# Attention features, mixture of experts and SoLU on one core: k and q stacks split in pairs of 64 partitions, and the upper part of k's features on another engine

## The chip, the core and the metric

The kernel runs on one core of a Trainium2 chip. The core has five engines with queues of their own: TensorE (PE, matrix multiplications, with weight loads shown as PEld), VectorE (DVE), ScalarE (ACT), GpSimd (POOL) and SyncE (SP, which here issues all transfers). The metric is device time in microseconds (us) of one execution; lower is better.

## What is computed

Three layers follow one another: random-feature attention over 4 batches of 8 heads, 576 positions and 64 dimensions with 128 features; a mixture of 8 experts in which each token takes one expert; and a SoLU layer with a layer norm.

```python
scale = 1.0 / np.sqrt(np.sqrt(D))
q_s, k_s = (q * scale, k * scale)
def phi(x):
    proj = np.einsum('bhsd,md->bhsm', x, omega)
    h = proj - np.sum(x * x, axis=-1, keepdims=True) / 2.0
    h = h - np.max(h, axis=-1, keepdims=True)
    return np.exp(h) / np.sqrt(m)
q_p, k_p = (phi(q_s), phi(k_s))
kv = np.einsum('bhsm,bhsd->bhmd', k_p, v)
z = np.sum(k_p, axis=2)
num = np.einsum('bhsm,bhmd->bhsd', q_p, kv)
den = np.einsum('bhsm,bhm->bhs', q_p, z)[..., None] + 1e-06
x = (num / den)          # then rows of 512: experts, then SoLU
```

The matrix products run in 16-bit floats, and every factor is split in an upper part (the value rounded to 16 bits) and a lower part (the rest), so that three products give nearly the precision of 32 bits.

## The kernel before, in words

There are three phases. Phase A is the attention, phase B the experts, phase C the SoLU layer. A and B are interleaved by hand: the program is one list of instructions for each engine, in the order in which the code is written (the pool manager orders nothing), and a piece of A is put between the steps of B.

Phase A (`stream_a`) is a list of units. A batch has nine k units (positions in four blocks of 128 and a tail, for two halves of the heads) and nine q units. The text calls one turn of the loop a slot, and it handles several units at once, each at another stage. In slot i, `feat_max` (DVE, tile `nm`) takes the maxima of unit i, `proj` (PE, tile `pj`) makes unit i + 1, `feat_exp` (ACT, tile `feat`, four instructions) makes the features of unit i, and `k_split` divides the features of unit i - 1, when it is a k unit, in `fh` (upper part) and `fl` (lower part); `k_acc` multiplies them with v on PE in slot i + 1. A q unit is transposed on PE instead, split by `q_split`, multiplied in `q_num` and divided in `q_norm`. Between batch 0 and batch 1 lie six slots without units (`GAP`).

`proj` takes its factors from stacks (tile `stk`): 128 partitions, of which 0 to 63 hold the upper and 64 to 127 the lower part of k or q of a pair of heads, in 1152 columns (two heads of 576 positions). One matrix product over the 128 partitions so takes both parts. A stack is made in three steps for batches 1 to 3. `load_pair` (lines 113 to 125) loads the pair from memory twice, once to each half of the partitions. `split_pair` (lines 127 to 139) first casts all of it to 16 bits on ACT (line 138), and then POOL subtracts, on the lower half alone, the cast from the loaded value (line 139, which stands at line 62 in the profile, in the helper `sub`). Batch 0 has its data in another layout and does not come to these lines. There are eight stacks a batch, four of k and four of q, so 24 in all. A table in `stream_a` (lines 387 to 397) says in which slot a stack is split: q of a batch in its slots 1, 3, 5, 7, k of the next batch in slots 11, 13, 15, 17 (six or seven more in batch 0). The load of the pair after next is put two slots behind each.

Phase B (`phase_b`) is a pass over one expert a batch: 16 passes of twelve products (lines 659 to 661) and eight of 24 (lines 676 to 678). ACT and DVE take their results out (`hh`, `hl`, lines 635 and 636; `yT`). Its weights come in 64 chunks (tile `wraw`, three buffers), each split by ACT (`wh`, line 546) and DVE (`wl`, line 547).

SP issues in program order. An instruction of SP that waits holds back all that stand behind it.

Of the kernel before, what the change touches and what calls it, by code (L numbers as in the profile page):

```python
# [8 lines left out]
F32 = mybir.dt.float32  # L9
F32R = mybir.dt.float32r  # L10
F16 = mybir.dt.float16
# [49 lines left out]
def sub(eng, out, a, b):  # L61
    eng.tensor_tensor(out=out, in0=a, in1=b, op=ALU.subtract)  # L62
# [3 lines left out]
def attn_moe_solu(ctx: ExitStack, tc, qk0, qT, kT, v, omT, w_gate, w1, w2, w_in, w_out, g_ln, out):  # L66
# [46 lines left out]
    def load_pair(b, which, pr):  # L113
        if b >= B:
            return
        if b == 0:
            n, cs = "qk".index(which), slice(512 * pr, min(512 * pr + 512, 4 * S))
            raws[b, which, pr] = raw0[n][:, cs]
            sp.dma_start(raws[b, which, pr], qk0[n, :, cs])
            return  # L120
        src = (qT if which == "q" else kT)[b - 1]
        r = ap_.tile([128, 2 * S], F32, name="raw", tag="raw", bufs=2)
        sp.dma_start(r[0:64], src[:, pr, :])
        sp.dma_start(r[64:128], src[:, pr, :])
        raws[b, which, pr] = r

    def split_pair(b, which, pr, fast=False):
        if b >= B:
            return
        dst = stacks[b, which, pr] = ap_.tile([128, 2 * S], F16, name="stk", tag="stk", bufs=8)  # L130
        r = raws.pop((b, which, pr))
        eng = dve if fast else pool
        if b == 0:
            n = r.shape[1]
            act.copy(dst[:, 0:n], r)
            sub(eng, dst[:, S:S + n], r, dst[:, 0:n])
        else:
            act.copy(dst, r)  # L138
            sub(eng, dst[64:128], r[64:128], dst[64:128])

    vraws = {}

# [76 lines left out]
    kvs = {}  # L219
    kvacc = {}  # L220

    def k_split(f):
        h, l = split_feat(f)
        dve.tensor_scalar(h, f, PSC, None, op0=ALU.mult)
        yield h, l
        dve.scalar_tensor_tensor(l, f, PSC, h, op0=ALU.mult, op1=ALU.subtract)  # L226

# [145 lines left out]
    def stream_a():  # L373
# [8 lines left out]
        def at(i, fn):  # L382
            later.setdefault(i, []).append(fn)

        for b in range(B):
            o = U * b + (GAP if b else 0)
            g = 0 if b else GAP
            stream = [(b, "q", i) for i in range(4)] + [(b + 1, "k", i) for i in range(4)]
            stream += [(b + 1, "q", i) for i in range(2)]
            for i in range(8):  # L390
                w = 2 * i + 1 if i < 4 else 2 * i + 3 + g + (b == 0 and i == 4)
                if b == 0 and i < 4:
                    continue
                if stream[i][0] < B:
                    at(o + w, lambda x=stream[i]: split_pair(*x))
                if (b or i >= 4) and stream[i + 2][0] < B:
                    at(o + w + 2, lambda x=stream[i + 2]: load_pair(*x))
            if b == 0:
                for i in range(5):
                    at(QS[i], lambda i=i: split_pair(0, "q", i))  # L400
                at(o + 7 + g, lambda x=stream: (load_pair(*x[4]), load_pair(*x[5])))
            if b + 1 < B:
                for i in range(5):
                    at(o + g + (7, 7, 7, 14, 15)[i], lambda b=b, i=i: load_v(b + 1, i))
                    at(o + g + (11 + (b == 0), 12, 13, 15, 16)[i], lambda b=b, i=i: split_v(b + 1, i))
                    at(o + g + (12 + (b == 0), 13, 14, 16, 17)[i], lambda b=b, i=i: split_v_lo(b + 1, i))
# [27 lines left out]
        while i < n or later or xq or xps or hls or routes:  # L434
# [55 lines left out]
            if i < n and units[i]:  # L490
                feats[i] = feat_exp(pj, nm)
            if unit(i - 1, "k"):
                ks = k_split(feats.pop(i - 1))
                hls[i - 1] = next(ks)
            if new_num:
                b, _, t, half = un
# [686 lines left out]
```

## Time and profile before

| | us |
|---|---|
| median of 3 runs | 569.41 (568.27 to 570.55) |
| the profiled execution | 571.53 |
| its span, first to last instruction | 569.6 |
| PE busy | 507.8 (89%) |
| DVE busy | 454.0 (80%) |
| ACT busy | 336.5 (59%) |
| POOL busy | 121.6 (21%) |
| chain that ended last | PE 45%, DVE 28%, ACT 13%, issue 7%, DMA 4% |

The span has two parts. Up to about 350 us the phases A and B run interleaved, and no engine is busy all the time; from 360 us on, PE is busy nearly without a break with phases B and C. Busy times are read stage by stage, since a share over the whole span mixes the two. A wait is put down to the work that came last before it, and the busy time of an instruction also has in it what held it up while it ran.

### The profile page before, as it was taken

Reading aid. Unit: us, or ns where it says so; the run is one execution under the profiler, and the core shown is the slowest. Engines: PE = TensorE matmul, PEld = TensorE weight load, DVE = VectorE, ACT = ScalarE, POOL = GpSimd, SP = SyncE. Lnnn points to the kernel's source line nnn. Section 1 sums busy time; section 2 is a strip of 40 time slices with the busy share of each in tenths; the row PEclk is TensorE's granted clock in tenths of the full one; section 3 lists DMA queues with packets and bytes.
Section 4 is the critical chain, followed back from the end, with each engine's and each line's share of the span. In section 5 each row is a group of like instructions: output and inputs, shape, how many; then the busy total and the mean of one; then the engine's idle time right before and its main releaser. Section 6 shows DMA issues by size and latency. Waiting matters only on the chain.

```text
span 569.6 us, 11746 instructions
## 1 busy us (share of the span) xinstructions
PE 507.8 (89%) x4440; PEld 344.5 (60%) x4440; DVE 454.0 (80%) x929; ACT 336.5 (59%) x742; POOL 121.6 (21%) x110
## 2 busy tenths in 40 slices
PE   6878677988868998979989978999999999999995
PEld 3656566767757887858867756664444444444443
DVE  6978999889987989786886787777779988878670
ACT  6668656788557885657565456434375646645520
POOL 4221333133330232310011233211112121211100
PEclk9999899999979999989998999999999999999998
DMA  7505744747554454611455545506678887676541
GB/s 255 149 18 175 221 99 102 197 100 201 149 151 117 112 163 124 181 57 57 143 158 174 165 130 184 166 2 145 182 164 229 177 229 164 161 211 150 148 111 43
DMA packets 72462, 83.48 MB, mean 147 GB/s; under 512 B 42192, under 2 KB 42832, under 8 KB 72400
## 3 DMA queue, kind: packets, MB, share of 16 engines
q1 hardware_dynamic: 72400, 82.68, 53.2%
q8 instruction: 36, 0.59, 0.5%
q14 instruction: 26, 0.21, 0.1%
HBM read 63.79 MB, written 9.44 MB: 129 GB/s over the span
## 4 chain that ended last, share of the span: by engine, by line
PE 45%; DVE 28%; ACT 13%; issue 7%; DMA 4%; SPq 1%; POOL 1%; ACTq 0%; DVEq 0%; POOLq 0%
DVE wl L547 5%; PE h L732 5%; PE o L799 5%; PE o L801 5%; PE o L800 5%; PE h L730 5%; PE h L731 5%; ACT feat L211 4%; DVE nm L205 3%; PE g L677 3%; PE g L676 3%; PE g L678 3%; DVE fl L226 2%; ACT wh L546 2%; ACT stk L138 2%
## 5 line engine op out<-in xcount | busy, mean ns | idle before, releaser
L211 ACT ACTIVATE feat<-pj,nm 128x128 f32<-128x128 f32 x288 | 82.8, 378 | 43.5 <-DVE nm L205 39.9
L62 POOL TENSOR_TENSOR stk<-raw,stk 64x1152 f16<-64x1152 f32 (+2 forms) x33 | 68.4, 2073 | 177.6 <-ACT stk L138 141.5
L659 PE MATMUL g<-xh,wh 128*128 128x288 f16 (+2 forms) x224 | 65.2, 291 | 15.0 <-DVE hl L636 13.9
L676 PE MATMUL g<-hh,wh 128*128 128x288 f16 (+2 forms) x256 | 73.4, 287 | 1.1 <-DVE hl L636 0.9
L677 PE MATMUL g<-hl,wh 128*128 128x288 f16 (+2 forms) x256 | 73.5, 287 | 0.4 <-DVE hl L636 0.4
L678 PE MATMUL g<-hh,wl 128*128 128x288 f16 (+2 forms) x256 | 73.5, 287 | 0.0
L547 DVE SCALAR_TENSOR_TENSOR wl<-wraw,wh 128x512 f16<-128x512 f32 x56 | 58.3, 1040 | 16.6 <-ACT wh L546 14.0
L661 PE MATMUL g<-xh,wl 128*128 128x288 f16 (+2 forms) x224 | 65.3, 292 | 0.0
L660 PE MATMUL g<-xl,wh 128*128 128x288 f16 (+2 forms) x224 | 65.3, 292 | 0.0
L799 PE MATMUL o<-woh,lh 128*128 128x512 f16 (+1 forms) x152 | 55.9, 368 | 0.3 <-ACT ob L802 0.3
L801 PE MATMUL o<-woh,ll 128*128 128x512 f16 (+1 forms) x152 | 55.9, 368 | 0.0
L800 PE MATMUL o<-wol,lh 128*128 128x512 f16 (+1 forms) x152 | 55.9, 368 | 0.0
L205 DVE TENSOR_REDUCE nm<-pj 128x4 f32<-128x512 f32 x72 | 49.0, 681 | 0.9 <-PE pj L191 0.8
L636 DVE SCALAR_TENSOR_TENSOR hl<-g,hh 128x288 f16<-128x288 f32 (+2 forms) x64 | 28.9, 452 | 19.1 <-ACT hh L635 18.7
L732 PE MATMUL h<-wih,yl 128*128 128x512 f16 x112 | 42.5, 379 | 0.9 <-POOL yl L62 0.9
L730 PE MATMUL h<-wih,yh 128*128 128x512 f16 x112 | 42.5, 379 | 0.0
L731 PE MATMUL h<-wil,yh 128*128 128x512 f16 x112 | 42.4, 379 | 0.0
L756 POOL TENSOR_TENSOR rs<-sc,neghalf 128x1 f32<-128x1 f32 x18 | 10.3, 573 | 148.1 <-DVE sc L754 148.1
L546 ACT ACTIVATE wh<-wraw 128x512 f16<-128x512 f32 x56 | 36.1, 644 | 4.2 <-PE g L677 4.2
L635 ACT ACTIVATE hh<-g 128x288 f16<-128x288 f32 (+2 forms) x64 | 26.7, 425 | 19.5 <-PE g L661 19.5
L827 ACT ACTIVATE wck<-wck 128x2048 f32<-128x2048 f32 x16 | 30.5, 1904 | 12.6 <-DMA wck<-in_w_dram 12.6
L660 PEld LDWEIGHTS <-wh 128*128 128x128 f16 x224 | 22.2, 99 | 22.9 <-issue 17.5
(181 smaller groups left out, 1251.8 us busy)
## 6 DMA issues: line engine op xcount, KB each, us to landing
wck<-in_w_dram SPq DMA_DIRECT2D x16, 1024.0 KB, 6.0
wraw<-in_w_dram SPq DMA_DIRECT2D x56, 256.0 KB, 2.8
raw<-in_kT_dram SPq DMA_DIRECT2D x24, 288.0 KB, 4.7
raw<-in_qT_dram SPq DMA_DIRECT2D x24, 288.0 KB, 4.6
out_dram<-ob SPq DMA_DIRECT2D x17, 256.0 KB, 2.2
vraw<-in_v_dram SPq DMA_DIRECT2D x16, 256.0 KB, 4.8
xd<-x SPq DMA_DIRECT2D x16, 256.0 KB, 4.6
craw<-in_w_in_dram SPq DMA_DIRECT2D x8, 512.0 KB, 4.0
```

Of the source, the lines that this page charges most:

```text
L211: act.activation(f[:, i, :], ps[:, i, :], AF.Exp, bias=nm[:, i:i + 1])
L547: dve.scalar_tensor_tensor(l, r, BS, h, op0=ALU.mult, op1=ALU.subtract)
L660: pe.matmul(ps, wh[:, c, :], xl[:, c, cs], start=False, stop=False)
L676: pe.matmul(ps, wh[:, k % 4, :], hh[:, k, cs], start=(k == 0), stop=False)
L677: pe.matmul(ps, wh[:, k % 4, :], hl[:, k, cs], start=False, stop=False)
L678: pe.matmul(ps, wl[:, k % 4, :], hh[:, k, cs], start=False, stop=(k == 7))
L730: pe.matmul(ps[:, n, :], h[:, c, :], cw["wih"][:, c, cs], start=(c == 0), stop=False)
L731: pe.matmul(ps[:, n, :], h[:, c, :], cw["wil"][:, c, cs], start=False, stop=False)
L732: pe.matmul(ps[:, n, :], l[:, c, :], cw["wih"][:, c, cs], start=False, stop=(c == 3))
L799: pe.matmul(ps, h[:, k, :], cw["woh"][:, k, cs], start=(k == 0), stop=False)
L800: pe.matmul(ps, h[:, k, :], cw["wol"][:, k, cs], start=False, stop=False)
L801: pe.matmul(ps, l[:, k, :], cw["woh"][:, k, cs], start=False, stop=(k == 7))
```

## The change

Four things change, all of them for batches 1 to 3 alone.

The load: the pair comes once, the first head to partitions 0 to 63, the second to 64 to 127, in 576 columns. There are three buffers of half the size in place of two.

The split: ACT casts 128 x 576 to the first half of a new tile `hlp`, and DVE (no longer POOL) subtracts 128 x 576 into its second half. Four transfers from SBUF to SBUF then put the stack together: for each of the two heads its upper part to partitions 0 to 63, and its lower part to 64 to 127.

The order: the cast stands one slot earlier than the split did, and the subtraction with its four transfers one slot behind the cast. The loads are one slot earlier too.

The features: `fh` of a k unit is made by ACT where DVE made it.

```diff
-        r = ap_.tile([128, 2 * S], F32, name="raw", tag="raw", bufs=2)
-        sp.dma_start(r[0:64], src[:, pr, :])
-        sp.dma_start(r[64:128], src[:, pr, :])
+        r = ap_.tile([128, S], F32, name="raw", tag="raw", bufs=3)
+        sp.dma_start(r[0:64], src[:, pr, 0:S])
+        sp.dma_start(r[64:128], src[:, pr, S:2 * S])
...
-        else:
-            act.copy(dst, r)
-            sub(eng, dst[64:128], r[64:128], dst[64:128])
+            return None
+        hl = ap_.tile([128, 2, S], F16, name="hlp", tag="hlp", bufs=3)
+        act.copy(hl[:, 0], r)
+
+        def rest():
+
+            sub(dve, hl[:, 1], r, hl[:, 0])
+            for o in range(2):
+                for n in range(2):
+                    sp.dma_start(dst[64 * n:64 * n + 64, S * o:S * o + S], hl[64 * o:64 * o + 64, n])
+        return rest
...
-    def k_split(f):
+    def k_split(f, b):
         h, l = split_feat(f)
-        dve.tensor_scalar(h, f, PSC, None, op0=ALU.mult)
+        if b:
+            act.activation(h, f, AF.Copy, scale=PSC)
+        else:
+            dve.tensor_scalar(h, f, PSC, None, op0=ALU.mult)
...
-                w = 2 * i + 1 if i < 4 else 2 * i + 3 + g + (b == 0 and i == 4)
+                w = 2 * i if i < 4 else 2 * i + 2 + g + (b == 0 and i == 4)
...
-                    at(o + w, lambda x=stream[i]: split_pair(*x))
+                    at(o + w, lambda x=stream[i], w=o + w: at(w + 1, split_pair(*x)))
```

Two k slots of batch 1 on DVE, before (`hl`, `wl` and `kvl` are lower parts of phase B's results, of weights and of the sums over k):

```order
L205 TENSOR_REDUCE nm<-pj 128x4
L636 SCALAR_TENSOR_TENSOR hl<-g_1516,hh 128x320
L547 SCALAR_TENSOR_TENSOR wl<-wraw,wh 128x512
L224 TENSOR_SCALAR fh<-feat 128x512
L226 SCALAR_TENSOR_TENSOR fl<-feat,fh 128x512
L250 SCALAR_TENSOR_TENSOR kvl<-kv,kvh 128x260
L205 TENSOR_REDUCE nm<-pj 128x4
L636 SCALAR_TENSOR_TENSOR hl<-g_1572,hh 128x320
L547 SCALAR_TENSOR_TENSOR wl<-wraw,wh 128x512
L224 TENSOR_SCALAR fh<-feat 128x512
L226 SCALAR_TENSOR_TENSOR fl<-feat,fh 128x512
```

The same two slots on DVE after (lines of the new file; the functions further down stand eight to eleven lines lower):

```order
L213 TENSOR_REDUCE nm<-pj 128x4
L647 SCALAR_TENSOR_TENSOR hl<-g_1552,hh 128x320
L558 SCALAR_TENSOR_TENSOR wl<-wraw,wh 128x512
L237 SCALAR_TENSOR_TENSOR fl<-feat,fh 128x512
L261 SCALAR_TENSOR_TENSOR kvl<-kv,kvh 128x260
L213 TENSOR_REDUCE nm<-pj 128x4
L647 SCALAR_TENSOR_TENSOR hl<-g_1607,hh 128x320
L558 SCALAR_TENSOR_TENSOR wl<-wraw,wh 128x512
L62 TENSOR_TENSOR hlp<-raw,hlp 128x576
L237 SCALAR_TENSOR_TENSOR fl<-feat,fh 128x512
```

`fh` is gone from each slot, and the subtraction of a pair stands ahead of `fl` in every second one.

ACT in the same place, before:

```order
L635 ACTIVATE hh<-g_1572 128x320
L546 ACTIVATE wh<-wraw 128x512
L211 ACTIVATE feat<-pj,nm 128x128 x4
L138 CAST stk<-raw 128x1152
L635 ACTIVATE hh<-g_1629 128x320
L546 ACTIVATE wh<-wraw 128x512
L211 ACTIVATE feat<-pj,nm 128x128 x4
```

And after:

```order
L646 ACTIVATE hh<-g_1552 128x320
L557 ACTIVATE wh<-wraw 128x512
L219 ACTIVATE feat<-pj,nm 128x128 x4
L233 ACTIVATE fh<-feat 128x512
L139 CAST hlp<-raw 128x576
L260 ACTIVATE kvh<-kv 128x260
L646 ACTIVATE hh<-g_1607 128x320
L557 ACTIVATE wh<-wraw 128x512
L219 ACTIVATE feat<-pj,nm 128x128 x4
L233 ACTIVATE fh<-feat 128x512
```

`fh` of the unit before stands behind the four `feat` of each slot, and the cast is half as wide.

SP in the first half of batch 1's k slots, before:

```order
L529 DMA wraw<-in_w_dram 128x512
L123 DMA raw<-in_qT_dram 64x1152
L124 DMA raw<-in_qT_dram 64x1152
L123 DMA raw<-in_qT_dram 64x1152
L124 DMA raw<-in_qT_dram 64x1152
L123 DMA raw<-in_qT_dram 64x1152
L124 DMA raw<-in_qT_dram 64x1152
L529 ISA
L529 DMA wraw<-in_w_dram 128x512
```

And after, from the same weight load on:

```order
L540 DMA wraw<-in_w_dram 128x512
L123 DMA raw<-in_qT_dram 64x576
L124 DMA raw<-in_qT_dram 64x576
L146 DMA stk<-hlp 64x576 x4
L123 DMA raw<-in_qT_dram 64x576
L124 DMA raw<-in_qT_dram 64x576
L146 DMA stk<-hlp 64x576 x4
L123 DMA raw<-in_qT_dram 64x576
L124 DMA raw<-in_qT_dram 64x576
L146 DMA stk<-hlp 64x576 x4
L540 ISA
L540 DMA wraw<-in_w_dram 128x512
```

Each stack adds four transfers to SP's queue, of which the first waits for the subtraction. The order on PE does not change, and POOL's list only loses the 24 subtractions.

## Rows read from the trace of the kernel before

**Rows 1.** The page: span, busy times, granted clock in 40 slices.

```profile
span 569.6 us, 11746 instructions
PE 507.8 (89%) x4440; PEld 344.5 (60%) x4440; DVE 454.0 (80%) x929; ACT 336.5 (59%) x742; POOL 121.6 (21%) x110
...
PEclk9999899999979999989998999999999999999998
```

**Rows 2.** Busy time by stage: length, PE, PEld, DVE, ACT, POOL, PEclk, DMA share, GB/s.

```profile
48.30:77.60 29.30, 20.39 (x242) 16.82 (x242) 25.70 (x62) 18.72 (x37) 9.83 (x4) 0.94 0.75 211
77.60:106.00 28.40, 23.30 (x284) 18.31 (x283) 26.70 (x51) 19.77 (x56) 9.49 (x4) 1.00 0.44 112
106.00:136.30 30.30, 25.89 (x324) 22.00 (x325) 25.47 (x56) 24.98 (x65) 7.57 (x4) 1.00 0.65 179
136.30:172.10 35.80, 27.29 (x367) 22.68 (x365) 33.01 (x70) 21.82 (x59) 12.07 (x5) 0.90 0.53 146
172.10:212.00 39.90, 38.34 (x442) 32.73 (x442) 33.59 (x81) 30.91 (x81) 7.67 (x4) 1.00 0.47 127
212.00:251.30 39.30, 33.92 (x444) 28.63 (x443) 33.64 (x77) 24.94 (x66) 11.66 (x5) 1.00 0.46 129
```

**Rows 3.** Single lines on DVE: duration in ns, shortest, median, longest.

```profile
L547 DVE SCALAR_TENSOR_TENSOR wl<-wraw,wh x56: 669/692/2443, 75.5 to 366.7; 128x512 f16<-128x512 f32 x56
...
L224 DVE TENSOR_SCALAR fh<-feat x36: 396/417/1949, 9.2 to 253.3; 128x512 f16<-128x512 f32 x36
...
L205 DVE TENSOR_REDUCE nm<-pj x72: 658/682/694, 7.0 to 285.2; 128x4 f32<-128x512 f32 x72
```

**Rows 4.** Timelines of POOL and of DVE at 102 us: start, duration.

```profile
101.99 2.38 POOL L62 TENSOR_TENSOR stk<-raw,stk 64x1152 f16<-64x1152 f32 x1 [4.97 <-ACT stk L138]
...
102.80 2.11 DVE L547 SCALAR_TENSOR_TENSOR wl<-wraw,wh 128x512 f16<-128x512 f32 x1
```

**Rows 5.** Groups on DVE in the k slots of batch 1, 2, 3 (two rows each).

```profile
L224 DVE TENSOR_SCALAR fh<-feat 128x512 f16<-128x512 f32 x8 | 6.3, 785 | 0.0
L547 DVE SCALAR_TENSOR_TENSOR wl<-wraw,wh 128x512 f16<-128x512 f32 x3 | 4.9, 1633 | 0.1
...
L547 DVE SCALAR_TENSOR_TENSOR wl<-wraw,wh 128x512 f16<-128x512 f32 x5 | 9.8, 1968 | 1.8 <-ACT wh L546 1.7
L224 DVE TENSOR_SCALAR fh<-feat 128x512 f16<-128x512 f32 x8 | 4.8, 602 | 0.1
...
L547 DVE SCALAR_TENSOR_TENSOR wl<-wraw,wh 128x512 f16<-128x512 f32 x8 | 8.6, 1074 | 2.9 <-ACT wh L546 2.8
L226 DVE SCALAR_TENSOR_TENSOR fl<-feat,fh 128x512 f16<-128x512 f32 x8 | 7.1, 893 | 0.4
```

**Rows 6.** Groups of the whole span by shape: busy us, mean ns, idle before.

```profile
L62 POOL TENSOR_TENSOR stk<-raw,stk 64x1152 f16<-64x1152 f32 x24 | 58.3, 2429 | 148.4 <-ACT stk L138 141.5 <-PE pj L200 6.9
L546 ACT ACTIVATE wh<-wraw 128x512 f16<-128x512 f32 x56 | 36.1, 644 | 4.2 <-PE g L677 4.2
L138 ACT CAST stk<-raw 128x1152 f16<-128x1152 f32 x24 | 28.1, 1170 | 0.0
L62 DVE TENSOR_TENSOR tl<-e,th 128x1024 f16<-128x1024 f32 x16 | 19.6, 1225 | 7.0 <-ACT th L782 7.0
```

**Rows 7.** Timelines of DVE and of ACT in one k slot of batch 1.

```profile
98.95 0.68 DVE L205 TENSOR_REDUCE nm<-pj 128x4 f32<-128x512 f32 x1
...
99.73 1.14 ACT L211 ACTIVATE feat<-pj,nm 128x128 f32<-128x128 f32 x4 [2.14 <-DVE nm L205]
```

**Rows 8.** Transfers (KB, median us to landing), SP's issue, and PE's first use.

```profile
raw<-in_qT_dram SPq DMA_DIRECT2D x24, 288.0 KB, 4.6
vraw<-in_v_dram SPq DMA_DIRECT2D x8, 128.0 KB, 4.2
...
102.76 0.60 SPq L124 DMA_DIRECT2D raw<-in_kT_dram  x1
...
104.42 0.23 PE L199 MATMUL pj<-ws,stk 128*128 128x128 f16 x1
```

More of the change, by code (lines that the diff above doesn't have):

```diff
@@ L492, in stream_a @@
             if unit(i - 1, "k"):
-                ks = k_split(feats.pop(i - 1))
+                ks = k_split(feats.pop(i - 1), units[i - 1][0])
                 hls[i - 1] = next(ks)
```

## The prediction

> **What bounds the kernel now.** I read the page first, then busy time by stage, cut where the maxima `nm` of a unit start: the gap (48.3 to 77.6 us), then k and q slots of batches 1, 2 and 3 in turn. The change acts only there; behind it PE runs phases B and C, which the change leaves alone, so a gain made in these stages moves all the rest by as much [rows 1, 2]. In the gap and in the k slots of batches 1 and 2 DVE is busy for 25.7 of 29.3, 26.7 of 28.4 and 33.0 of 35.8 us, with PE at 20.4, 23.3 and 27.3: DVE sets the pace. In the q slots of batch 2 PE is busy for 38.3 of 39.9 us: there nothing that DVE saves comes out. The k slots of batch 3 lie between (PE 33.9 and DVE 33.6 of 39.3), and the q slots of batch 1 load ACT and DVE alike (25.0 and 25.5 of 30.3) [rows 2].
>
> But DVE is not working in all of this busy time. Three lines show it [rows 3]. `wl` takes 692 ns at the median and up to 2443; `fh` takes 417 and up to 1949; `nm`, which reads its values from PE's accumulators and not from SBUF, never takes over 694. The timelines say what holds the long ones: POOL's subtraction for a stack runs from 101.99 to 104.37 us, and the `wl` that starts at 102.80 ends with it, after 2.11 us [rows 4]. So an instruction of DVE that takes two inputs, or one at the fast rate, from SBUF stands still until POOL is done. ACT's cast releases POOL just when ACT turns to the next `wh`, so that `wl` falls in POOL's 2.4 us again and again.
>
> **What goes.** POOL's 24 subtractions of 2.43 us [rows 6], and with them DVE's standstill. By stage, against the medians of rows 3: k slots of batch 1, 8 x (785 - 417) + 3 x (1633 - 692) = 5.8 us; of batch 2, 5 x (1968 - 692) + 8 x (602 - 417) = 7.9; of batch 3, 8 x (1074 - 692) + 8 x (893 - 692) = 4.7 [rows 3, 5]. The gap has four of the 24 too [rows 2]; by batch 1's price they cost 0 to 5.8. The q slots have few hits. DVE also loses 27 `fh` of 417 ns, 11.3 us, nine in each stretch of k slots, and ACT half of each cast: 1170 ns for 1152 columns, about 0.65 for 576, so 12 us over 24 [rows 6].
>
> **What comes, on DVE and ACT.** DVE gets 24 subtractions of 128 x 576. The nearest row is `tl`, the same operation on 1024 columns in 1225 ns; with `wl` at 692 for 512 that is 1.04 ns a column, so 0.76 us each, 18 us in all, 3 in every stage of four pairs [rows 3, 6]. Its bounds are 0.69 (the `wl` of 512) and 1.23. ACT gets 27 `fh`; the nearest row is `wh`, the same shape with a scale, 644 ns, so 17.4 us [rows 6]. Net, DVE has 6.6, 8.7 and 5.5 us less to do in the three stretches of k slots (0.417 x 9 + 5.8, 7.9 or 4.7, less 3), and ACT gets 3.7 more in each (0.644 x 9, less 0.52 x 4).
>
> **The new wait.** `fh` on DVE needed nobody; on ACT it stands behind the four `feat`, and these wait for `nm`. DVE's `fl` now waits for `fh`, and the next `nm` stands behind `fl`. That is one ring for every k slot: `nm` 0.68, hand-over 0.1, `feat` 1.14, `fh` 0.6, `fl` 0.69, in all 3.2 us [rows 3, 5, 7]. While DVE does `fl` and `nm`, ACT has 1.3 us for `hh`, `wh` and the cast; `wh` and the cast take 0.65 each, so when all three come in one slot the ring grows by `hh`, to some 3.6. What now stands between `nm` and `fl` on DVE (`hl`, `wl`, the subtraction) hides under `feat` and `fh`. So no k slot can be shorter than 3.2 us, and this takes back part of what the standstill returns:
> - k slots of batch 1: now 28.4, without standstill 22.6, so the ring sets them. The first of the nine has no k unit before it; eight to nine rings are 25.6 to 28.8, I take 27.4: **-1.0**.
> - of batch 2: now 35.8, without standstill 27.9; nine rings are 28.8, and some slots were over 3.2 anyway: 28.8 to 33, I take 31.5: **-4.3**.
> - of batch 3: now 39.3, without standstill 34.6, and PE alone is busy for 33.9: 34 to 36.5, I take 35.0: **-4.3**.
> - the gap: DVE gets 3 us of subtractions and loses up to 5.8 of standstill; ACT waits for v there too. **-1.5** (-3 to +2).
> - q slots of batch 1: 3 us more on DVE, 2 less on ACT and few hits: **0** (-1 to +2). Of batch 2: PE sets them, DVE has 1.6 us to spare for 3 more: **+0.5** (0 to +2). Of batch 3: no stacks, no change.
>
> **The transfers.** A stack's transit was POOL's 2.4 us. Now DVE's 0.76 is followed by four issues of SP, up to 0.6 each (half-partition transfers in the rows), and by a landing: 4.2 to 4.6 us in the rows of loads from memory [rows 8]; the rows have no transfer inside SBUF, so 2.4 (POOL's own time) to 4.6. From the subtraction's start to the last landing that is 5.6 to 7.8 us. For k stacks and the first three of q there are two slots or more in hand. The fourth stack of q is subtracted in slot 7 and wanted by `proj` in slot 9: two slots of 3.2, 6.4 us, and in batch 1 PE takes its stack at 104.42, 0.05 us behind POOL's end, so without slack already [rows 4, 8]. Price: 0 to 1.4 us a batch, with a busy queue more: **+1.5** (0 to +4). Behind the waiting first transfer on SP stand weight loads. ACT never waited for such a load in 56 times (its idle time before `wh` goes to PE) [rows 6], so SP's extra two microseconds a stack cost nothing while three buffers stand ahead; if that cover were gone, 2 us a stack would come on ACT's path. Transfer load is no matter: the DMA share is 0.44 to 0.75 [rows 2], and the bytes loaded halve while as many are moved inside SBUF.
>
> The Trainium skill speaks against this form. Its page DMA: Bandwidth & Descriptors, section Rules for kernel authors, advises not to cut a transfer in two partition halves, since both use the same 16 engines and serialize; its section Anatomy of one DMA puts a fixed cost of some 2 us on each. By it four would follow one another for about 4 x (2.0 + 0.17) = 8.7 us, an estimate from that page, and the fourth q stack would be some 3 us late in each batch, about 568 in all. Against that, two loads issued 0.6 us apart both land in 4.2 to 4.6 [rows 8], so the fixed part overlaps.
>
> **The sum.** -1.0 - 4.3 - 4.3 - 1.5 + 0.5 + 1.5 = -9.1 us. The profiled execution took 571.53, with a span of 569.6 and so 1.9 outside it; it would become 562.4. It stands 2.1 over the median of the runs shown, 569.41, and by that median the time is **560.3**, say 560.5.
>
> **The rivals.**
> - *The ring doesn't bind, DVE's time comes out whole.* Standstill (18.4 in k slots, 3 in the gap), `fh` (11.3) and casts, less 18 of subtractions: about -18, 551. For it: PE's granted clock averages 0.90 in batch 2's k slots [rows 2], so it stood at the lower level there for a while, and a steadier PE would win that back. Against: the ring follows from the program's order.
> - *Late stacks eat most of it.* Transfers that queue behind loads come 3 us late in each batch at the fourth q stack, or some k stack waits too: +9, 566 to 571. For it: batch 1 has no slack. Against: the q slots of batches 2 and 3 come later.
> - *ACT becomes the bound in k slots: slower.* The place is the 27 k slots. If ACT's `hh`, `wh` and cast do not fit under `fl` and `nm`, and PE's next pass, which waits for `hl`, drifts with them, a slot takes 3.6 plus a wait for PE, about 4.2; 27 x 4.2 = 113 against the 103.5 that these stages take now gives +10, and with gap and lateness 580. It decides from 3.8 us a slot on. For it: ACT would have 25 us of work in 31. Against: ACT's work in a slot, 1.14 + 0.6, `hh` of at most 0.65, and `wh` and the cast in every second slot, is about 3.0.
> - *The standstill doesn't go*, since DVE itself now does the work: no row says that DVE stands for anything but POOL, so I give it no chance of its own.
>
> **How the numbers follow.** The forecast (554 to 566) gets 0.48, whole relief (544 to 554) 0.20, late stacks 0.18, ACT as bound 0.14. About 0.5% is what a measurement of this kernel can tell from no change: under 566.6 is faster, over 572.3 slower. Faster is 0.48 + 0.20 less the slow edge, 0.66; same 0.20; slower 0.14. The range for 8 in 10 leaves out half of whole relief and most of the slow case: 549 to 573. Most of the chance is on one side, so the forecast's own range is the one given with it.
>
> **What would show it.** In the profile after, `wl` and `fh` or `fl` in k slots should have no duration over 0.75 us before phase A ends; DVE's subtraction some 0.76; `fh` on ACT some 0.62, and ACT no longer idle for `nm` but DVE's `fl` idle for `fh`: the ring. The stretches of k slots should take about 27, 31 and 35 us, q slots of batch 2 still about 40. PE waiting for a transfer of `stk` at the tenth or eleventh unit of a batch would show lateness. I am wrong if k slots take over 3.8 us, if PE waits for stacks by over 3 us a batch, or if the subtraction takes over 1.2.

## The result, and the profile after

The changed kernel takes 562.93 us (median of 4 runs, 561.29 to 563.70) against 569.57 before (also 4 runs, 568.27 to 570.55): 0.9874 of the time before, 95% interval 0.9851 to 0.9898, so some 7 us less. The profiled execution took 563.37 us with a span of 561.5.

The page, to be held against [rows 1] (and its line on the transfers: KB, median us to landing):

```profile
span 561.5 us, 11966 instructions
PE 506.7 (90%) x4440; PEld 344.8 (61%) x4440; DVE 432.3 (77%) x926; ACT 339.3 (60%) x769; POOL 63.0 (11%) x86
...
PEclk8998989798999999999999999999999999999999
...
stk<-hlp SPq DMA_DIRECT2D x96, 72.0 KB, 2.3
```

DVE has lost 21.7 us of busy time (454.0 to 432.3) and POOL 58.6; ACT is nearly where it was (336.5 to 339.3), since the 17.5 us of upper parts that it gained are for the most part made up for by the casts, which lost 11.5 (28.1 before [rows 6], 16.6 after). The transfers land 2.3 us after their issue at the median. The groups of DVE and ACT from 0 to 285 us show the parts one by one:

```profile
L237 DVE SCALAR_TENSOR_TENSOR fl<-feat,fh 128x512 f16<-128x512 f32 x36 | 27.3, 758 | 16.3 <-ACT fh L233 15.2
L558 DVE SCALAR_TENSOR_TENSOR wl<-wraw,wh 128x512 f16<-128x512 f32 x37 | 25.6, 691 | 4.1 <-ACT wh L557 2.9 <-DMA stk<-hlp 0.7
L62 DVE TENSOR_TENSOR hlp<-raw,hlp 128x576 f16<-128x576 f32 x24 | 18.0, 750 | 0.2
...
L233 ACT ACTIVATE fh<-feat 128x512 f16<-128x512 f32 x27 | 17.5, 648 | 0.8 <-PE num L286 0.8
L139 ACT CAST hlp<-raw 128x576 f16<-128x576 f32 x24 | 16.6, 690 | 5.0 <-DMA raw<-in_kT_dram 5.0
```

`wl` is back at its own length, 691 ns on average in these stages where it reached 1633 and 1968 in single stretches before [rows 5]; the standstill is gone. In its place `fl` stands idle for 15.2 us until ACT has written `fh`: the ring. The stages, cut where the `nm` of their first unit starts, against [rows 2] (length, PE, PEld, DVE, ACT, POOL, PEclk, DMA share, GB/s):

```profile
48.80:77.20 28.40, 21.10 (x233) 17.17 (x233) 23.48 (x67) 16.61 (x37) 0.00 (x0) 0.88 0.73 220
77.20:104.30 27.10, 23.39 (x283) 18.43 (x281) 20.70 (x46) 22.17 (x64) 0.00 (x0) 1.00 0.52 143
104.30:139.40 35.10, 29.16 (x334) 24.81 (x335) 25.75 (x59) 24.58 (x67) 0.00 (x0) 0.87 0.47 133
139.40:169.70 30.30, 25.52 (x368) 21.83 (x367) 24.89 (x66) 23.09 (x65) 0.00 (x0) 0.98 0.65 184
169.70:210.20 40.50, 38.84 (x444) 32.94 (x444) 34.88 (x83) 30.68 (x83) 0.00 (x0) 1.00 0.45 133
210.20:246.70 36.50, 33.41 (x442) 28.43 (x440) 27.37 (x74) 26.14 (x72) 0.00 (x0) 1.00 0.49 140
```

| stage | before | after | difference | forecast |
|---|---|---|---|---|
| gap | 29.3 | 28.4 | -0.9 | -1.5 |
| k slots, batch 1 | 28.4 | 27.1 | -1.3 | -1.0 |
| q slots, batch 1 | 30.3 | 35.1 | **+4.8** | 0, and a share of the +1.5 for late stacks |
| k slots, batch 2 | 35.8 | 30.3 | -5.5 | -4.3 |
| q slots, batch 2 | 39.9 | 40.5 | +0.6 | +0.5, and a share of the +1.5 |
| k slots, batch 3 | 39.3 | 36.5 | -2.8 | -4.3 |
| all that follows | 318.3 | 314.8 | -3.5 | 0 |

With 0.5 us more ahead of the gap the spans differ by 8.1. One stage went the other way, the q slots of batch 1. Two waits and a lower clock in it are new. SyncE's issues and PE's waits there (start, duration, and in brackets the idle time before):

```profile
100.19 1.38 SPq L157 DMA_DIRECT2D vraw<-in_v_dram  x3
101.68 3.13 SPq L146 DMA_DIRECT2D stk<-hlp  x4
```

```profile
107.21 0.27 PE L207 MATMUL pj<-ws,stk 128*128 128x128 f16 x1 [3.20 <-DMA stk<-hlp]
```

VectorE's subtraction for the fourth q stack ends at 100.5, but SP is issuing three loads of `v`; the four transfers follow from 101.68 on, the last at 104.23, and PE waits 3.20 us for them. From 106.5 on, 0.7 us before that wait ends, the granted clock is at half, which is the level of 1.2 GHz, for 6.8 us, and full again after it (columns as in the stages; the middle row):

```profile
100.00:106.50 6.50, 3.54 (x44) 2.87 (x42) 5.03 (x9) 5.35 (x16) 0.00 (x0) 1.00 0.75 216
106.50:113.30 6.80, 5.87 (x51) 4.93 (x52) 1.38 (x2) 2.28 (x8) 0.00 (x0) 0.50 0.41 125
113.30:120.00 6.70, 6.70 (x73) 5.65 (x72) 5.57 (x12) 6.48 (x19) 0.00 (x0) 1.00 0.29 72
```

The waits of the whole span name SP once more (who waits for whom, us in total, times, longest):

```profile
SPq L146 <- DVE hlp L62: 25.2, 13, 4.5
...
ACT v_h L171 <- DMA vraw<-in_v_dram: 8.6, 5, 2.7
```

SP stands 25.2 us at the transfers until VectorE has subtracted (at the second of each four; the first takes the cast alone), and what is queued behind, the loads of `v` above all, goes out later: ACT waits 8.6 us for `v`. The same waits in the kernel before:

```profile
ACT v_h L163 <- DMA vraw<-in_v_dram: 2.4, 2, 1.3
...
ACT v_h L167 <- DMA vraw<-in_v_dram: 1.6, 1, 1.6
```

### The profile page after: what moved, and what is told of

It is laid out like the page before. It is cut to its first block, busy times and chain, and to the rows that moved or that the text cites. A ratio compares the mean times of both kernels' runs of the same rounds, so it can differ in the third digit from the quotient of the medians.

```text
span 561.5 us, 11966 instructions
## 1 busy us (share of the span) xinstructions
PE 506.7 (90%) x4440; PEld 344.8 (61%) x4440; DVE 432.3 (77%) x926; ACT 339.3 (60%) x769; POOL 63.0 (11%) x86
## 4 chain that ended last, share of the span: by engine, by line
PE 50%; DVE 21%; ACT 11%; DMA 7%; issue 6%; SPq 3%; POOL 1%; ACTq 0%; DVEq 0%; POOLq 0%
PE h L743 5%; PE o L810 5%; PE o L812 5%; PE o L811 5%; PE h L741 5%; PE h L742 5%; ACT feat L219 4%; DVE nm L213 4%; PE g L687 3%; PE g L688 3%; PE g L689 3%; PE g L670 2%; PE g L672 2%; PE g L671 2%; DMA vraw<-in_v_dram 2%
## 5 line engine op out<-in xcount | busy, mean ns | idle before, releaser
L558 DVE SCALAR_TENSOR_TENSOR wl<-wraw,wh 128x512 f16<-128x512 f32 x56 | 42.3, 756 | 12.2 <-ACT wh L557 8.9
L237 DVE SCALAR_TENSOR_TENSOR fl<-feat,fh 128x512 f16<-128x512 f32 x36 | 27.3, 758 | 16.3 <-ACT fh L233 15.2
L62 POOL TENSOR_TENSOR wil<-ctmp,wih 128x512 f16<-128x512 f32 x8 | 9.3, 1158 | 272.2 <-ACT wih L626 272.2
L207 PE MATMUL pj<-ws,stk 128*128 128x128 f16 x216 | 31.3, 224 | 4.5 <-DMA stk<-hlp 3.4
L751 DVE TENSOR_REDUCE sc<-h 128x1 f32<-128x1024 f32 x18 | 21.9, 1218 | 16.8 <-PE h L743 16.8
```

## Experiments

My theory was: the gain is the end of VectorE's standing; the ring holds the k slots at 3.1 us and takes part of it back; SP's order of the transfers and of the loads of `v` costs the rest. Its rivals were: the lighter work is the gain and not the standing, the ring only follows another limit, and the transfers hold one another up. Times, each with its ratio to the kernel before on the same chip:

| kernel | us | ratio (95% interval) |
|---|---|---|
| changed kernel | 562.93 | 0.9874 (0.9851 to 0.9898) |
| e1: three loads of v later | 560.05 | 0.9820 (0.9798 to 0.9842) |
| e2: upper part ahead of the exponentials | 554.25 | 0.9736 (0.9683 to 0.9790) |
| e3: upper part on VectorE | 558.62 | 0.9789 (0.9762 to 0.9817) |
| e4: GpSimd busy besides | 578.47 | 1.0148 (1.0106 to 1.0191) |
| e5: before, subtraction on VectorE | 580.16 | 1.0195 (1.0170 to 1.0220) |
| e6: before, upper part on ScalarE | 570.18 | 1.0002 (0.9981 to 1.0023) |
| e7: e2 with v's loads moved | 546.07 | 0.9589 (0.9569 to 0.9609) |
| e8: transfers from GpSimd's queue | 558.85 | 0.9795 (0.9759 to 0.9832) |
| e9: changed kernel without transfers | 577.09 | 1.0110 (1.0083 to 1.0137) |
| e10: e7 with GpSimd's queue | 546.39 | 0.9575 (0.9547 to 0.9604) |
| e11: e3 with v's loads moved | 550.75 | 0.9654 (0.9626 to 0.9681) |
| e12: changed, v's loads moved | 556.57 | 0.9780 (0.9734 to 0.9825) |

### The place of v's loads on SyncE (e1, e12, e8)

e1:

```diff
-                    at(o + g + (7, 7, 7, 14, 15)[i], lambda b=b, i=i: load_v(b + 1, i))
+                    at(o + g + (8, 8, 8, 14, 15)[i], lambda b=b, i=i: load_v(b + 1, i))
```

> The changed kernel with one number altered: the first three loads of v of the next batch are issued one unit later, so that on SyncE they stand behind the four transfers of the fourth q stack and no longer ahead of them. Theory (the transfers come late because SP is held by the v loads ahead of them): in batch 1 the four transfers are issued some 1 us sooner, TensorE's wait of 3.2 us at the second projection of the q slots shrinks to about 2, the clock may or may not stay up behind it, and the time is 560 to 562.5 against 562.9. Rival (the four transfers hold one another up on the DMA engines, whatever SP does): the wait stays above 2.8 and the time within 0.5 of 562.9.

It took 560.05. The four transfers are issued from 100.70 on. PE's wait for them goes from 3.20 us to 0.8 (the row below has it for the whole span), less than the 2 that the theory gave, and the clock stays at full where it fell before (e1: the wait, then the same window and the stage of the q slots of batch 1):

```profile
PE pj L207 <- DMA stk<-hlp: 1.3, 3, 0.5
...
106.50:113.30 6.80, 6.80 (x78) 5.66 (x77) 4.00 (x7) 5.05 (x16) 0.00 (x0) 1.00 0.67 200
...
104.70:136.60 31.90, 27.09 (x334) 22.79 (x335) 25.59 (x59) 24.29 (x67) 0.00 (x0) 0.96 0.58 167
```

The stage is 31.9 us long and no longer 35.1. PE records 27.09 us for 334 matmuls in it, and 29.16 for as many in the changed kernel: the lower clock costs 2.1 us of PE's time. That `v`'s loads ahead of the transfers make the stack late is shown; the rival that the four transfers hold one another up, whatever SP does, fell. Whether they do it by holding up SP's issue (1.0 us sooner here) or on the way (landing 1.0 us shorter), e8 tells below. The page DMA: Bandwidth & Descriptors of the Trainium skill, section Rules for kernel authors, says that transfers to two partition halves serialize. Here a stack's four take 0.6 us each to issue and land after 2.3 at the median, and the slow ones of batch 1 (median 4.3) got shorter, 3.3, as soon as 768 KB of `v` stood behind them: these times fit engines shared with other loads, and not that four cost four times one.

e12 has all of `v`'s loads moved, the last two ahead of the transfers of their slots:

```diff
-                    at(o + g + (7, 7, 7, 14, 15)[i], lambda b=b, i=i: load_v(b + 1, i))
+                    at(o + g + (8, 8, 8, 13, 14)[i], lambda b=b, i=i: load_v(b + 1, i))
```

> The changed kernel with v's loads alone moved as in the fastest run (the first three one unit later, the last two one unit earlier), the upper part on ScalarE behind the exponentials as changed. Theory (v's place on SyncE is worth the same 8 us in each order of the features: 554.3 to 546.1 with the upper part first, 558.6 to 550.8 with it on VectorE): 553 to 557, and by difference the last two loads alone some 5. Rival (the ring hides what the loads cost, so that only the 2.9 us of the first three remain): 559 to 561.

556.57, in the theory's range, and ACT's wait for `v` falls from 8.6 to 2.5 us:

```profile
ACT v_h L171 <- DMA vraw<-in_v_dram: 2.5, 2, 1.4
```

The q slots of batch 1 (103.38 to 133.34 us here) take 30.0 us, so the place of `v`'s loads is by itself worth all that this stage had lost. The two edits together are worth 0.0094 of the time before, some 5.4 us; in the other two orders of the features it is 0.0147 (e2 to e7) and 0.0135 (e3 to e11), some 8. That it is smaller here fits the ring, which sets the k slots, but e12's interval is too wide to tell 5 from 7.

e8 takes the transfers off SP altogether:

```diff
-                    sp.dma_start(dst[64 * n:64 * n + 64, S * o:S * o + S], hl[64 * o:64 * o + 64, n])
+                    pool.dma_start(dst[64 * n:64 * n + 64, S * o:S * o + S], hl[64 * o:64 * o + 64, n])
```

> The changed kernel with the transfers within SBUF issued by GpSimd's queue in place of SyncE's; GpSimd has nothing else to do there. Theory (SyncE stands at the transfers until VectorE's subtraction is done, 25 us in all, and v and the weights queue behind it): that wait is gone from SyncE, TensorE's wait for the fourth q stack of batch 1 falls from 3.2 to under 2, ScalarE's waits for v from 8.6 to under 4, and the time is 557 to 560.5. Rival (GpSimd issues more slowly, so that the stacks come later still and TensorE waits for them in all batches): 563 to 570.

558.85 is in the theory's range, but only half of its reasons hold. ACT's wait for `v` falls from 8.6 to 2.3 us, and the gap from 28.4 to 25.6, where the load of k that ACT waited for (5.0 us, the row of L139 above) now costs it 0.8. PE's wait for the fourth q stack does not shrink (e8: the wait, and the time to landing, shortest, median, longest, of the 96 transfers):

```profile
PE pj L207 <- DMA stk<-hlp: 4.8, 2, 3.0
```

```profile
DMA to landing us min/median/max: 1.9/2.8/7.5
```

From SP the same row reads 1.9, 2.3 and 5.2. The Trainium skill's page SBUF — State Buffer, section SBUF: two separate sides, warns that a transfer from GpSimd's queue waits while VectorE holds the ports that both use. The longer landings agree in their direction; that this is their cause was not tested, and for the fourth q stack of batch 1 another is nearer. Its last three transfers are issued from 97.54 on, 0.3 us behind the subtraction, so no queue held them up. But SP issues three loads of `v` from 96.99 on, and the three transfers land 6.1 to 7.5 us after their issue. The seven that the same queue issues from 83 to 94 us land after 1.9 to 2.7, and in e10 below, with `v` moved out of the way, the four of this stack land after 2.5 to 3.2. So in e8 the wait comes from the 768 KB of `v` that are under way at the same time, and not from SP's issue; in the changed kernel both were there.

### The ring, and the engine of the upper part (e2, e3, e11)

e2 turns ScalarE's order in a unit round:

```diff
+            if unit(i - 1, "k"):
+                ks = k_split(feats.pop(i - 1), units[i - 1][0])
+                hls[i - 1] = next(ks)
             if i < n and units[i]:
                 feats[i] = feat_exp(pj, nm)
-            if unit(i - 1, "k"):
-                ks = k_split(feats.pop(i - 1), units[i - 1][0])
-                hls[i - 1] = next(ks)
```

> The changed kernel with ScalarE's order inside a k unit turned round: the upper part of the last unit's features is written before this unit's exponentials, not behind them, so that the ring maximum, exponentials, upper part, lower part, maximum is open (the upper part is written while VectorE takes this unit's maximum). Theory (the ring sets the 3.1 us of a k slot): the k slots of batch 1 fall from 3.1 to 2.5 to 2.8, its k stretch from 27.1 to 23 to 25.5, those of batches 2 and 3 lose 1 to 3 each, and the time is 556 to 560. Rival (another engine's sum sets the slot and the ring only follows it): slots stay at 3.0 to 3.1 and the time within 1.5 of 562.9.

554.25, below the theory's range, and the k slots of batch 1 take 23.1 us, those of batch 2 26.4 and of batch 3 34.4, against 27.1, 30.3 and 36.5 (the row of batch 1, columns as in the stages):

```profile
78.30:101.40 23.10, 22.80 (x288) 18.68 (x287) 20.44 (x46) 21.62 (x65) 0.00 (x0) 1.00 0.55 150
```

First the ring of the changed kernel, from DVE's and ACT's timelines of one slot (in order of time):

```profile
88.28 0.68 DVE L213 TENSOR_REDUCE nm<-pj 128x4 f32<-128x512 f32 x1
...
90.75 0.69 DVE L237 SCALAR_TENSOR_TENSOR fl<-feat,fh 128x512 f16<-128x512 f32 x1 [1.39 <-ACT fh L233]
91.36 0.68 DVE L213 TENSOR_REDUCE nm<-pj 128x4 f32<-128x512 f32 x1
```

```profile
89.06 1.14 ACT L219 ACTIVATE feat<-pj,nm 128x128 f32<-128x128 f32 x4 [0.93 <-DVE nm L213]
90.08 0.65 ACT L233 ACTIVATE fh<-feat 128x512 f16<-128x512 f32 x1
```

Each waits for the one before, and the next `nm` comes 3.08 us later. Then the same place in e2, DVE first:

```profile
88.19 0.68 DVE L213 TENSOR_REDUCE nm<-pj 128x4 f32<-128x512 f32 x1
88.79 0.48 DVE L647 SCALAR_TENSOR_TENSOR hl<-g,hh 128x320 f16<-128x320 f32 x1
89.19 0.68 DVE L237 SCALAR_TENSOR_TENSOR fl<-feat,fh 128x512 f16<-128x512 f32 x1
89.79 0.68 DVE L213 TENSOR_REDUCE nm<-pj 128x4 f32<-128x512 f32 x1
```

```profile
87.90 0.64 ACT L233 ACTIVATE fh<-feat 128x512 f16<-128x512 f32 x1
88.91 1.14 ACT L219 ACTIVATE feat<-pj,nm 128x128 f32<-128x128 f32 x4 [0.37 <-DVE nm L213]
```

`fh` was written while DVE still had other work, `fl` waits for nothing, and this slot, which has no `wl` in it, takes 1.6 us; the nine take 2.6 each on average. `fl`'s wait for `fh` is 0.7 us in the whole span. The ring was a limit of its own: shown.

e3 leaves the ring out in another way, with the upper part where it was before:

```diff
-        if b:
-            act.activation(h, f, AF.Copy, scale=PSC)
-        else:
-            dve.tensor_scalar(h, f, PSC, None, op0=ALU.mult)
+        dve.tensor_scalar(h, f, PSC, None, op0=ALU.mult)
```

> The changed kernel with the upper part of k's features back on VectorE in all batches; the stacks stay as changed (cast of 128x576, subtraction on VectorE, transfers). Theory (the gain is that VectorE no longer stands behind GpSimd; moving the upper part buys little since the ring takes its place): 561.5 to 565, k stretch of batch 1 26 to 28, no operation of VectorE over its own length. Rival (VectorE's load in the k slots was the bound and the 11.3 us taken from it are the gain): 567 to 571, each k stretch of batches 1 to 3 some 3 longer than in the changed kernel.

558.62: below both ranges. With 27 more operations on DVE (busy 440.4 us, 8.1 more) the kernel is faster by 0.0085 of the time before, 4.8 us; the k slots of batch 1 take 24.8 and not 27.1, of batch 2 28.1 and not 30.3. So this half of the change, in the order in which it was made, is a loss beside the new stacks. e11 asks what it is worth where the ring is open and `v` comes in time (the edits of e3 and e12 together):

> The changed kernel with v's loads moved as in the fastest run, and the upper part of k's features on VectorE in all batches as before the change. Against the fastest run this isolates the upper part's engine where the ring is open. Theory (with the ring open, ScalarE's taking the upper part is a gain of VectorE's time): slower than 546.1, at 549 to 553. Rival (the upper part's engine is worth nothing in either order, only the ring cost something): 545 to 548.

550.75 against 546.07 of e7, the same but for the upper part's engine and order: there the move to ScalarE is a gain of 0.0065, 3.7 us. The engine was right, the place in its order was wrong: with `v`'s loads moved in the same way and the upper part behind the exponentials, e12 is 0.0126 slower than e11, some 7 us.

### What the stacks gain (e4, e5, e9, e6)

e4 keeps the changed kernel and makes GpSimd work beside it (`spare` is a tile that nothing reads):

```diff
+    spare = const.tile([64, 2, S], F16, name="spare")
...
             sub(dve, hl[:, 1], r, hl[:, 0])
+            for o in range(2):
+                sub(pool, spare[:, o], r[64:128], hl[64:128, 0])
```

> The changed kernel with GpSimd doing, for each of the 12 pair stacks of the later batches that are split in this way, two subtractions of 64x576 beside VectorE's, written to a tile that nothing reads; nothing else waits for them but the buffers they read. So GpSimd is as busy as before the change and nothing in the path needs it. Theory (GpSimd's subtractions hold VectorE's instructions up): operations of VectorE of two to three times their length come back in the k slots, 10 to 20 us of them in all, and the time goes to 567 to 574. Rival (the gain came from lighter work and not from the end of the standing): 562 to 564.

(The stacks split in this way are 24 and not 12: GpSimd does 48 of these, 69.1 us of work against 58.3 before the change [rows 6].) 578.47, worse than the theory's range. DVE's busy time goes from 432.3 to 450.5 with the same work; the groups from 0 to 285 us, to be held against the ones above, show where:

```profile
L561 DVE SCALAR_TENSOR_TENSOR wl<-wraw,wh 128x512 f16<-128x512 f32 x35 | 31.1, 888 | 3.4 <-ACT wh L560 2.3 <-DMA stk<-hlp 0.6
...
L62 DVE TENSOR_TENSOR hlp<-raw,hlp 128x576 f16<-128x576 f32 x24 | 21.8, 908 | 0.3
```

The kernel is 0.0274 of the time before slower than the changed one, some 15.6 us, beside 18.2 us more on DVE. That the buffers which the spare work reads come free later is not the reason: nothing but one load waits for it, 0.6 us. That GpSimd alone, with work that nobody needs, holds VectorE up is shown. It is the rule of the Trainium skill's page SBUF — State Buffer, section SBUF: two separate sides: the two engines share a pair of ports that one of them has for a whole instruction; this trace agrees, with 888 ns on average for a `wl` of 691.

e5 should then have brought most of the gain with one word in the kernel before:

```diff
-            sub(eng, dst[64:128], r[64:128], dst[64:128])
+            sub(dve, dst[64:128], r[64:128], dst[64:128])
```

> The kernel before with one word altered: the subtraction of the later batches' stacks (64x1152, in place in the stack) goes to VectorE in place of GpSimd. No transfers, the cast still 128x1152 on ScalarE, the upper part of the features still on VectorE, the raw stack still loaded twice. Cost by estimate 24 times 1.3 to 1.5 us on VectorE, from the 0.75 us that 576 columns take in the changed kernel. Theory (most of the gain is the end of VectorE's standing behind GpSimd, and the split over 64 partitions pairs with its transfers adds only the saved casts): 559 to 564. Rival (the shorter casts and subtractions carry the gain): 566 to 571.

580.16: slower than before, and out of both ranges. Two things, in its rows (the group of the subtraction from 0 to 285 us, then DVE's and ACT's timelines in one k slot):

```profile
L62 DVE TENSOR_TENSOR stk<-raw,stk 64x1152 f16<-64x1152 f32 x24 | 32.5, 1355 | 18.3 <-ACT stk L138 13.5 <-issue 4.6
```

```profile
94.12 0.68 DVE L205 TENSOR_REDUCE nm<-pj 128x4 f32<-128x512 f32 x1
...
97.16 1.36 DVE L62 TENSOR_TENSOR stk<-raw,stk 64x1152 f16<-64x1152 f32 x1 [1.21 <-issue]
98.55 0.69 DVE L226 SCALAR_TENSOR_TENSOR fl<-feat,fh 128x512 f16<-128x512 f32 x1
99.16 0.68 DVE L205 TENSOR_REDUCE nm<-pj 128x4 f32<-128x512 f32 x1
```

```profile
95.91 1.17 ACT L138 CAST stk<-raw 128x1152 f16<-128x1152 f32 x1
```

The subtraction stands right behind its cast, so DVE waits 18.3 us for it, and `nm` of the next unit behind both: this slot takes 5.0 us. And the standing was never larger than the work that replaces it: DVE is busy 457.6 us, 32.5 of them with the subtraction, so 425.1 without; against 454.0 before, the standing cost 28.9.

e9 takes away the first of these, with the changed kernel's one unit between cast and subtraction, and leaves the second:

```diff
...
-        hl = ap_.tile([128, 2, S], F16, name="hlp", tag="hlp", bufs=3)
-        act.copy(hl[:, 0], r)
-        def rest():
-            sub(dve, hl[:, 1], r, hl[:, 0])
-            for o in range(2):
-                for n in range(2):
-                    sp.dma_start(dst[64 * n:64 * n + 64, S * o:S * o + S], hl[64 * o:64 * o + 64, n])
-        return rest
+        act.copy(dst, r)
+        return lambda: sub(dve, dst[64:128], r[64:128], dst[64:128])
```

(and `load_pair` as in the kernel before.)

> The changed kernel with its times and orders, the upper part on ScalarE, and VectorE's subtraction one unit behind the cast, but the stacks made as before: raw loaded twice, cast 128x1152, subtraction 64x1152 in place (1.355 us each by the run with this subtraction straight behind the cast), no transfers. Against the changed kernel it costs 24 times 0.6 us of VectorE and some 12 us of ScalarE, and saves the transfers and the waits for them. Theory (the pairs of 64 partitions are worth their transfers, since VectorE and ScalarE stand in the ring in the k slots): 564 to 570. Rival (the transfers take back all that the pairs save, so that the gain was only the subtraction's new engine and place): 558 to 563.

577.09, slower than the theory's range, and slower than before. Its groups of the two operations from 0 to 285 us:

```profile
L62 DVE TENSOR_TENSOR stk<-raw,stk 64x1152 f16<-64x1152 f32 x24 | 32.5, 1355 | 0.9 <-issue 0.3
```

```profile
L138 ACT CAST stk<-raw 128x1152 f16<-128x1152 f32 x24 | 28.0, 1167 | 2.9 <-DMA raw<-in_kT_dram 2.9
```

DVE's wait at the subtraction is 0.9 us in all, so this time it is the work: 1355 ns for each of 24 in place of 750, and the cast of 1167 in place of 690. So taking GpSimd's work to VectorE gains nothing at the old size; it is the pairs of 64 partitions, with half the columns for the same stack, that make it a gain, and with their 96 transfers counted they are worth 0.0236 of the time before, some 13 us. My theory that the end of the standing is by itself most of the gain fell.

e6 is the other half of the change, alone:

```diff
-    def k_split(f):
+    def k_split(f, b):
         h, l = split_feat(f)
-        dve.tensor_scalar(h, f, PSC, None, op0=ALU.mult)
+        if b:
+            act.activation(h, f, AF.Copy, scale=PSC)
+        else:
+            dve.tensor_scalar(h, f, PSC, None, op0=ALU.mult)
...
-                ks = k_split(feats.pop(i - 1))
+                ks = k_split(feats.pop(i - 1), units[i - 1][0])
```

> The kernel before with the other half of the change alone: the upper part of k's features on ScalarE from batch 1 on, the stacks cast and subtracted as before, on GpSimd. Theory, by the run with the upper part back on VectorE (this half costs some 4 us where ScalarE writes it behind the exponentials): 570 to 576 against 570. Rival (this half is a gain where VectorE is held up by GpSimd, since it takes 11.3 us from the engine that is late): 563 to 568.

570.18 against 569.23, 1.0002: no difference, at the lower end of what the theory gave. Its profile has both sides: DVE is busy for 439.4 us and not 454.0, and `fl` stands idle for `fh` for 16.9 us, while `wl` still takes 1130 ns on average up to 285 us. That these two cancel is the likely reading; no run takes them apart.

### The combinations (e7, e10)

e7 has the edits of e2 and e12.

> The changed kernel with ScalarE's order turned round as in the run where the upper part goes first, and with v's loads moved on SyncE: the first three one unit later (behind the fourth q stack's transfers), the last two one unit earlier (ahead of the transfers of that unit). Theory (the two late arrivals in the q slots of batch 1, the fourth q stack and v, are SyncE's doing and add to the ring): the q slots of batch 1 take 31 to 33 us against 35.1, the time is 549 to 552.5. Rival (the gain of 2.9 with v's loads behind the transfers does not add to the ring's 8.7, since what was waited for there is then waited for elsewhere): 553 to 556.

546.07, better than the theory's range: 0.9589 of the time before, 0.0285 (16 us) below the changed kernel. The k slots and the q slots of batch 1, in the slowest of its four executions (548.16):

```profile
75.20:98.30 23.10, 22.41 (x280) 18.07 (x278) 20.34 (x46) 21.47 (x64) 0.00 (x0) 1.00 0.58 156
98.30:128.10 29.80, 26.77 (x356) 23.59 (x355) 25.45 (x58) 24.71 (x68) 0.00 (x0) 1.00 0.58 165
```

PE is busy for 22.41 of 23.1 us in the k slots, where it had 5 us to wait before [rows 2], and the q slots take 29.8 and not 35.1. Apart, the ring (e2) and the loads (e12) are worth 0.0138 and 0.0094 of the time before, 0.0232; together they are worth 0.0285, so neither hides the other.

> The fastest so far (upper part first, v's loads moved: 546.1) with the transfers issued by GpSimd's queue in place of SyncE's. Theory (SyncE still stands 16.7 us at the transfers in it, and the gap lost 3 us less with GpSimd's queue): 542 to 546. Rival (what SyncE held up was v and the fourth stack, which moving v has already mended): 545.5 to 549.

e10 (e7 with the edit of e8) took 546.39, a ratio of 0.9575 against 0.9589: the same within the intervals. The rival holds: what came late by SP's order was `v` and the fourth stack, and e7 has mended both.

## Why the prediction was right, and where its steps were not

The forecast was 560.5 in a range of 549 to 573, and faster; measured, 562.93. By the profiled execution the forecast was 562.4 and the time 563.37. The sum is good to a microsecond, the terms are not, and that it came out so close is luck: the six stages of the change gave -5.1 us where -9.1 was forecast, and -3.5 came from the part behind them, where nothing was forecast. By the medians the gain is some 7 us.

- **The standstill** goes, as said: `wl` at 691 ns, the subtraction at 750 (forecast 760), the upper part on ACT 648 (forecast 644). Its size was well read too: some 18 us in the k slots and up to 5.8 in the gap forecast, 28.9 on all of DVE by e5. In the three stretches of k slots DVE is busy for 6.0, 8.1 and 6.3 us less, where 6.6, 8.7 and 5.5 were forecast. What the prediction did not see is that its end is worth nothing unless the new subtraction is shorter than the standing: it has both terms, 18 us of subtractions at 0.76, and they are right, but e5 and e9 show how much hangs on that size.
- **The ring** was right in mechanism and length: 3.2 us forecast, 3.1 measured, with `fl` idle for `fh`. Of its signs one was wrong: ACT is still idle for `nm`, as the timeline of the ring shows (0.93 us), since in a ring each waits for the other. It was counted only as something that takes back a part; e3 shows that with it the whole move of the upper part is a loss beside the new stacks. k slots of batches 1 and 2 came as forecast or better (-1.3 and -5.5 for -1.0 and -4.3). Of batch 3 the term was too large: -2.8 for -4.3, since the ring costs 2 us there as well (36.5 against 34.4 in e2) and not the 0.4 that was put on top of 34.6.
- **Late stacks** came as feared, but in batch 1 alone: 3.2 us there and none in batches 2 and 3, against 0 to 1.4 each. The step that named the slack of batch 1 as nought was right; it did not see that three loads of `v` stand ahead of the transfers on SP. Nor was transfer load "no matter" there: its shares of 0.44 to 0.75 are averages of whole stages, and e8 has the transfers land late for `v`'s loads alone. By the prediction's own mark, a wait for stacks of over 3 us a batch, it was wrong in this batch.
- **The q slots of batch 1** are the mis-sized term: 0 (-1 to +2) forecast, +4.8 measured. The step that failed is the one on SP, that its extra time at a stack costs nothing. It looked at the weight loads behind the transfers, which have buffers in hand, and left out `v`'s loads, the last two of which have one slot; and it priced PE's wait without the lower clock that came with it. e1 and e12 take the stage to 31.9 and 30.0 us by nothing but the place of these loads.
- **All that follows** was taken as 0 and gave -3.5. The next two stretches, first of the kernel before, then of the changed one (columns as in the stages):

```profile
251.30:289.00 37.70, 36.67 (x404) 30.89 (x403) 30.12 (x71) 24.05 (x69) 1.16 (x1) 0.96 0.33 102
289.00:353.00 64.00, 55.29 (x496) 42.98 (x495) 48.37 (x111) 32.82 (x70) 15.40 (x13) 0.97 0.51 159
```

```profile
246.70:282.80 36.10, 35.06 (x404) 30.08 (x403) 29.66 (x70) 24.66 (x71) 1.16 (x1) 1.00 0.33 103
282.80:345.00 62.20, 53.68 (x497) 41.94 (x495) 48.07 (x110) 32.66 (x69) 15.41 (x13) 1.00 0.52 164
```

  In both PE is busy for 1.6 us less with as many matmuls, at a clock of 1.00 for 0.96 and 0.97: the lower clock fell elsewhere. The other runs say that this goes with the execution and not with the change. From the first `nm` of batch 3's q slots to the end, with the same work, the fourteen profiled executions take 314.2 to 318.3 us. It is 314.7 in e9 and 315.8 in e5, which are slower than the kernel before, and 317.5 in e10, among the fastest. Why the clock fell in one execution and not in another stays open.
- **The rivals.** The ring didn't leave whole relief room, but e2, where it is open, came to 554, near that rival's 551. ScalarE as the bound did not come: the three stretches of k slots take 93.9 us and not 113. The Trainium skill's rule on partition halves (DMA: Bandwidth & Descriptors, Rules for kernel authors) would have made 568, with the fourth q stack some 3 us late in each batch. Batch 1 had 3.2, but e1 takes it to 0.8 with the same four transfers, and batches 2 and 3 had none. The section that the prediction takes the 2 us from (Anatomy of one DMA) is on transfers from GpSimd's queue, and these go out from SyncE.

## What to carry to other kernels

When an operation moves to another engine, follow the round trip of its result, not the engines' sums: with `v` in time, the same move lost some 7 us behind the exponentials (e12 against e11) and gained 3.7 ahead of them (e7 against e11). When work moves off an engine that holds another up, what counts is whether the work that replaces it is shorter than the holding up (18.0 us against 28.9 here; 32.5 was a loss). A new wait on a queue that issues transfers is paid by whatever is queued behind it with the least slack, so list all of it, not only the largest; and ask what else is under way when a transfer is wanted, since a stage's average does not show it.

## What the hardware showed that was not expected

A transfer of 72 KB within SBUF, from and to 64 partitions, lands 2.3 us after its issue at the median (1.9 to 5.2), about as soon as a load of 256 KB of weights (2.8), and the time rose to 3.4 to 5.2 with three loads of `v` ahead of it. Issued from GpSimd's queue the same transfers needed 2.8 at the median and up to 7.5, the latter right behind three loads of `v`. And with a wait of 3.2 us of PE came 6.8 us at half the clock, from 0.7 us before its end on; PE's work in that stage took 29.16 us and not 27.09 as in e1.
